# Moving a tile's query transpose, and a new batch's pooling, to other slots of a hand-written order

## The chip, the cores and the metric

The kernel runs on one core of a Trainium2 chip. The metric is device time in microseconds (us), the median of several executions. A core has engines that run side by side, each through its own instructions in order: TensorE (PE in the profile, with its weight loads as PEld), VectorE (DVE), ScalarE (ACT), GpSimd (POOL) and SyncE (SP). SP and POOL issue the DMAs of this kernel. An instruction that waits for a semaphore holds up whatever stands behind it on its engine, and that is true of a DMA's issue as well.

## What is computed

Attention over pooled keys and values, then a mixture of four experts over its output. Keys and values are averaged over groups of 8 rows, so 576 queries of a head see 72 keys.

```python
# q, k, v: (8 batches, 8 heads, 576 tokens, 64)
k_p = k.reshape(B, H, Sp, pool, D).mean(axis=3)      # Sp = 72
v_p = v.reshape(B, H, Sp, pool, D).mean(axis=3)
scores = scale * np.matmul(q, k_p.transpose(0, 1, 3, 2))
scores = scores - np.max(scores, axis=-1, keepdims=True)
attn = np.exp(scores)
attn = attn / (np.sum(attn, axis=-1, keepdims=True) + 1e-09)
x = np.matmul(attn, v_p)                             # heads side by side: (4608, 512)

p = domain_probs / (domain_probs.sum(-1, keepdims=True) + 1e-09)
for e in range(4):
    h = np.maximum(x @ w1[e], 0.0)                   # 512 -> 1024
    out += p[:, e:e + 1] * (h @ w2[e])               # 1024 -> 512
```

## The kernel before

**Tiles, groups, steps.** The 4608 tokens are 36 tiles of 128; four tiles make a group of 512, nine groups in all. A batch has 4.5 tiles, so some tiles hold rows of two batches. A *step* s is one expert of one group (36 steps). The main loop (line 603) walks through the steps, twelve *slots* each. In every three slots, two make an eighth of the hidden layer of step s+1 (`up`, four matmuls each, line 429) and one makes the output of one tile of step s (`down`, eight matmuls, line 462, followed by `collect` on DVE, which scales and adds into `acc`, and after the last expert stores `acc` from SP, line 485).

**The attention in the gaps.** The attention of later tiles is hung onto the slots by a plan, a dictionary from a slot's number to functions. At a slot the loop first emits the matmuls of the slot and then the planned functions, in the order in which they were put in. The schedule is manual: this emission order is the order on every engine. For a tile t of group g = 2 to 8 (t = g*4 + i), `base = (4g - 5 + i) * 12`, so successive tiles are twelve slots apart. `plan_tile(t, base - 2, turn)` puts in:

- `turn_q` at `base - 2 + turn`: `qT`, the transposed queries, by a transposing DMA from SP (line 290) that reads `qrow`; for t = 8 `turn` is 0;
- `scores` and `less_max` at `base`: the matmuls of line 306 with `qT` and the batch's `kT`, then on DVE the maximum (line 317) and the subtraction (line 319);
- `expo` on ACT (line 329) and `attn_T` at `base + 1`: `attnT`, the transposed probabilities, by a transposing DMA from SP (line 368);
- `sums` at `base + 2`: three DVE instructions (lines 350 to 353);
- `context` at `base + 6`: x's product (line 386) with `attnT` and the batch's `vbd`, then `x_sb` on DVE (line 392), then a transposing DMA from SP to `xT` (line 406), which the up-projection of the tile's group reads;
- `gate` at `base + 6`: POOL copies one element of `x_sb` (line 501), so that what stands behind it on POOL leaves only then; behind it `load_q` of tile t + 4 (line 107).

Tiles 0 to 7 are transposed on TensorE in place of by DMA.

**A new batch.** `plan_batch(b, slot)` is called for the first tile that holds rows of batch b (tiles 9, 13, 18, 22, 27 and 31 for batches 2 to 7), before that tile's `plan_tile`. It puts in `prep_k` (four DVE instructions: two folds at line 225, one at 232, the masked copy `kpad` at 240), `prep_kT` (a transposing DMA from SP, line 249) and `prep_v` (five DVE instructions, to `vbd`). The raw keys and values of batch b + 2 are loaded by POOL (lines 79 and 83) at slot `base + 6` of that tile and of the next, so behind `gate` and `load_q`.

Of the kernel before, what the change touches and what calls it, by code (L numbers as in the profile page):

```python
# [17 lines left out]
def kernel(  # L18
# [23 lines left out]
    TPG = G // P  # L42
# [104 lines left out]
    for sign, base in ((1, 0), (-1, SP - 1)):  # L147
        nc.gpsimd.affine_select(
            out=own[:], in_=own[:], compare_op=ALU.is_ge, fill=0.0,
            base=base, channel_multiplier=sign,  # L150
# [133 lines left out]
    def by_dma(t):  # L284
        return t >= 2 * TPG
# [202 lines left out]
    SLOTS = 12  # L488
    plan = {}

    def at(slot, fn, *args):
        plan.setdefault(slot, []).append((fn, args))

    def plan_batch(b, slot):
        at(slot, prep_k, b)
        at(slot + 4, prep_kT, b)
        at(slot + 8, prep_v, b)


    def gate(t):  # L500
# [2 lines left out]
    def plan_tile(t, slot, turn=0):  # L503
        exp, norm, move, sum_v = (3, 4, 3, 8) if by_dma(t) else (4, 5, 8, 10)
        if t + TPG < NT and not by_dma(t):
            at(slot, load_q, t + TPG)
        at(slot + turn, turn_q, t)
        at(slot + 2, scores, t)
        at(slot + 2, less_max, t)
        at(slot + exp, expo, t)  # L510
        at(slot + move, attn_T, t)
        at(slot + norm, sums if by_dma(t) else normalise, t)
        at(slot + sum_v, context, t)
        if by_dma(t):
            at(slot + sum_v, gate, t)
            if t + TPG < NT:
                at(slot + sum_v, load_q, t + TPG)
# [10 lines left out]
    for g in range(2, NG):  # L528
        for i in range(TPG):
            t = g * TPG + i  # L530
            base = (E * g - 5 + i) * SLOTS
            last_b = ((t + 1) * P - 1) // S
            if last_b >= done_batches:
                plan_batch(last_b, base - 13)
                done_batches += 1
                if last_b + 2 < B:
                    waiting += [(load_k, last_b + 2), (load_v, last_b + 2)]
            plan_tile(t, base - 2, -4 if t > 2 * TPG else 0)
            if waiting:
                load, b = waiting.pop(0)  # L540
                at(base + 6, load, b)
# [103 lines left out]
```

## Time and profile before

| | |
|---|---|
| time, median of 3 runs | 561.85 us (561.16 to 562.88) |
| the profiled execution: its time | 563.63 us |
| its span on the core | 561.7 us |
| granted TensorE clock, mean | 0.996 |
| `up` matmuls, line 429 | 271.8 us busy, 379 ns each |
| `down` matmuls, line 462 | 269.9 us busy, 379 ns each |
| query transposes on SP, line 290 | 27, median 3.8 us from issue to landing |
| probability transposes, line 368 | 28, median 2.6 us |
| x transposes, line 406 | 28, median 2.5 us |
| key transposes, line 249 | 6, median 2.6 us |
| loads of raw keys, 512 KB (POOL) | 7, median 8.1 us |
| loads of raw values, 512 KB (POOL) | 8, median 8.6 us |

The profile is one execution. For each engine it has what ran when, and the idle time in front of an instruction with the one whose end released it. A busy time is a sum over an engine's instructions; a wait counts for the whole only where the engine that waits sets the pace. The chain that ended last is followed back from the last instruction, at each step to what released it. For a DMA, "to landing" runs from its issue to its last completion.

### The profile page before, as it was taken

Reading aid. Unit: us, or ns where it says so; the run is one execution under the profiler, and the core shown is the slowest. Engines: PE = TensorE matmul, PEld = TensorE weight load, DVE = VectorE, ACT = ScalarE, POOL = GpSimd, SP = SyncE. Lnnn points to the kernel's source line nnn. Section 1 sums busy time; section 2 is a strip of 40 time slices with the busy share of each in tenths; the row PEclk is TensorE's granted clock in tenths of the full one; section 3 lists DMA queues with packets and bytes.
Section 4 is the critical chain, followed back from the end, with each engine's and each line's share of the span. In section 5 each row is a group of like instructions: output and inputs, shape, how many; then the busy total and the mean of one; then the engine's idle time right before and its main releaser. Section 6 shows DMA issues by size and latency. Waiting matters only on the chain.

```text
span 561.7 us, 7210 instructions
## 1 busy us (share of the span) xinstructions
PE 533.6 (95%) x2837; PEld 259.4 (46%) x2892; DVE 267.7 (48%) x458; ACT 210.8 (38%) x352; POOL 71.8 (13%) x121
## 2 busy tenths in 40 slices
PE   3799999999999898998999899999999999999997
PEld 1564554444444344444444344444444444444443
DVE  5865856444644445543563344744474444422222
ACT  1555553333333333333333233333333333333330
POOL 7224311210111000121011100110010000000000
PEclk9899999999999999999999999999999999999999
DMA  9999995544545335376535553334332331110001
GB/s 141 207 204 200 203 103 127 78 61 65 109 69 74 62 75 83 40 83 84 102 56 78 78 101 58 53 40 79 73 46 35 77 68 29 25 47 37 1 0 75
DMA packets 110688, 45.30 MB, mean 81 GB/s; under 512 B 87584, under 2 KB 106016, under 8 KB 110656
## 3 DMA queue, kind: packets, MB, share of 16 engines
q0 software_dynamic: 52512, 22.55, 32.8%
q1 hardware_dynamic: 58144, 22.30, 17.7%
q8 instruction: 22, 0.36, 0.3%
q14 instruction: 10, 0.08, 0.0%
HBM read 45.16 MB, written 9.44 MB: 97 GB/s over the span
## 4 chain that ended last, share of the span: by engine, by line
PE 88%; DMA 7%; DVE 2%; issue 1%; ACT 1%; POOL 0%; DVEq 0%; POOLq 0%
PE o_ps L462 41%; PE h_ps L429 40%; DMA qT<-qrow 5%; PE sc L306 2%; PE x_ps L386 2%; PE h_ps L445 2%; DMA kraw<-in_k_dram 1%; DMA attnT<-attn 1%; PE x_ps L412 1%; DVE kraw L225 0%; ACT attnT L373 0%; PE qT_ps L296 0%; PE o_ps L551 0%; POOL kraw L79 0%; DVE mx L317 0%
## 5 line engine op out<-in xcount | busy, mean ns | idle before, releaser
L433 ACT ACTIVATE h_sb<-h_ps 128x512 bf16<-128x512 f32 x280 | 166.5, 597 | 297.1 <-PE h_ps L429 290.6
L429 PE MATMUL h_ps<-xT,w 128*128 128x512 bf16 x1088 | 271.8, 379 | 1.5
L462 PE MATMUL o_ps<-w,h_sb 128*128 128x512 bf16 x1129 | 269.9, 379 | 1.4
L462 PEld LDWEIGHTS <-h_sb 128*128 128x128 bf16 x1152 | 112.3, 98 | 133.5
L477 DVE SCALAR_TENSOR_TENSOR acc<-o_ps,p_sb,acc 128x512 f32<-128x512 f32 x108 | 80.9, 749 | 179.0 <-PE o_ps L462 176.3
L429 PEld LDWEIGHTS <-w 128*128 128x128 bf16 x1120 | 105.9, 98 | 116.8
L501 POOL COPY gated<-x_sb 1x1 bf16<-1x1 bf16 x28 | 7.8, 278 | 370.6 <-DVE x_sb L392 370.6
L473 DVE TENSOR_SCALAR acc<-o_ps,p_sb 128x512 f32<-128x512 f32 x36 | 27.0, 749 | 58.3 <-PE o_ps L462 58.3
L317 DVE TENSOR_REDUCE mx<-sc 128x8 f32<-128x576 f32 x36 | 27.2, 754 | 19.3 <-PE sc L306 19.3
L107 POOL DMA_DIRECT2D qrow<-in_q_dram x36 | 30.4, 846 | 21.6 <-DMA w<-in_moe_w_dram 11.5
L319 DVE TENSOR_TENSOR d_sb<-sc,mx 128x576 f32<-128x576 f32 x36 | 27.3, 757 | 1.2
L392 DVE SCALAR_TENSOR_TENSOR x_sb<-x_ps,rs 128x512 bf16<-128x512 f32 x28 | 19.4, 692 | 16.4 <-PE x_ps L386 16.4
L329 ACT ACTIVATE attn<-d_sb 128x576 bf16<-128x576 f32 x28 | 19.1, 682 | 13.2 <-DVE d_sb L319 10.8
L306 PE MATMUL sc<-kT,qT 128*128 128x144 bf16 (+1 forms) x160 | 15.3, 230 | 7.6 <-DMA qT<-qrow 6.8
L350 DVE TENSOR_REDUCE es<-attn 128x8 f32<-128x576 bf16 x28 | 20.9, 745 | 0.5
L306 PEld LDWEIGHTS <-qT 128*128 128x128 bf16 (+1 forms) x160 | 10.7, 101 | 17.9 <-DMA qT<-qrow 9.7
L386 PEld LDWEIGHTS <-attnT 128*128 128x128 bf16 (+1 forms) x155 | 11.6, 100 | 9.1 <-DMA attnT<-attn 3.1
L386 PE MATMUL x_ps<-vbd,attnT 128*128 128x192 bf16 (+5 forms) x155 | 14.2, 231 | 1.5 <-DMA attnT<-attn 1.5
L225 DVE TENSOR_TENSOR kraw<-kraw 128x1280 bf16<-128x1280 bf16 (+5 forms) x18 | 10.8, 599 | 3.0 <-DMA kraw<-in_k_dram 2.7
L225 DVE TENSOR_TENSOR vraw<-vraw 128x1280 bf16<-128x1280 bf16 (+1 forms) x16 | 10.4, 652 | 0.2
L255 PE MATMUL kT_ps<-ident,kpad 128*128 128x128 bf16 x10 | 1.2, 264 | 9.3 <-DVE kpad L240 9.3
L445 PE MATMUL h_ps<-xT,w 128*128 128x128 bf16 x128 | 9.3, 240 | 0.7 <-ACT xT L418 0.7
(61 smaller groups left out, 153.4 us busy)
## 6 DMA issues: line engine op xcount, KB each, us to landing
out_dram<-acc SPq DMA_DIRECT2D x36, 256.0 KB, 2.0
vraw<-in_v_dram POOLq DMA_DIRECT2D x8, 512.0 KB, 8.6
w<-in_moe_w_dram POOLq DMA_DIRECT2D x8, 512.0 KB, 16.4
w<-in_moe_w_dram POOLq DMA_DIRECT2D x4, 1024.0 KB, 16.7
kraw<-in_k_dram POOLq DMA_DIRECT2D x7, 512.0 KB, 8.1
qrow<-in_q_dram POOLq DMA_DIRECT2D x28, 128.0 KB, 4.1
kraw<-in_k_dram POOLq DMA_DIRECT2D x2, 256.0 KB, 4.0
kraw<-in_k_dram POOLq DMA_DIRECT2D x8, 64.0 KB, 7.5
```

The source lines that it names most:

```text
L107: nc.gpsimd.dma_start(out=qrow[t][at:at + n], in_=q[b][:, tok:tok + n, :].rearrange("h p d -> p h d"),)
L225: nc.vector.tensor_add(out=rows[:, i0:i1, 0:w], in0=rows[:, i0:i1, 0:w], in1=rows[:, i0:i1, w:2 * w],)
L306: nc.tensor.matmul(sc[at:at + n, pair // 2, (pair % 2) * PW:(pair % 2 + 1) * PW], lhsT=qT[t][:, pair, at:at + n], rhs=kT[b][:].rearrange(" ...
L317: nc.vector.reduce_max(out=mx[:], in_=view, axis=AX.X)
L319: nc.vector.tensor_tensor(out=d_sb[:], in0=view, in1=mx[:].unsqueeze(3).to_broadcast([P, 2, 4, SP]), op=ALU.subtract,)
L350: nc.vector.reduce_sum(out=es[:], in_=e, axis=AX.X)
L386: nc.tensor.matmul(ps[at:at + n, h0 * D:(h0 + c1 - c0) * D], lhsT=attnT[t][:, i, at:at + n], rhs=flat[:, c0 * D:c1 * D], start=(i == 0), s ...
L429: nc.tensor.matmul(ps[:], lhsT=w1_sb[e][:, kc, fb * P:(fb + 1) * P], rhs=xT[g][:, kc, :], start=(kc == 0), stop=(kc == KC - 1),)
L433: nc.scalar.activation(out=hs[s][:, fb, :], in_=ps[:], func=ACT.Relu)
L462: nc.tensor.matmul(ps[:], lhsT=hs[s][:, fb, i * P:(i + 1) * P], rhs=w2_sb[e][:, fb, :], start=(fb == 0), stop=(fb == FB - 1),)
L473: nc.vector.tensor_scalar_mul(out=accs[t][:], in0=ps[:], scalar1=p_sb[:, e, t:t + 1])
L477: nc.vector.scalar_tensor_tensor(out=accs[t][:], in0=ps[:], scalar=p_sb[:, e, t:t + 1], in1=accs[t][:], op0=ALU.mult, op1=ALU.add,)
```

## The change

```diff
     def plan_batch(b, slot):
-        at(slot, prep_k, b)
-        at(slot + 4, prep_kT, b)
-        at(slot + 8, prep_v, b)
+        at(slot + 5, prep_k, b)
+        at(slot + 8, prep_kT, b)
+        at(slot + 9, prep_v, b)
...
             if last_b >= done_batches:
-                plan_batch(last_b, base - 13)
+                plan_batch(last_b, base - 2 - SLOTS)
...
-            plan_tile(t, base - 2, -4 if t > 2 * TPG else 0)
+            plan_tile(t, base - 2, -9 if t > 2 * TPG else 0)
```

In slots counted from the tile's `base`:

| what | slot before | slot after | stands behind, in the slot after |
|---|---|---|---|
| `turn_q` of tile t (t = 9 to 35) | base - 6 | base - 11 | `attn_T` of tile t - 1 |
| `prep_k` of a new batch | base - 13 | base - 9 | (`sums` of tile t - 1 are at base - 10) |
| `prep_kT` | base - 9 | base - 6 | `context`, `gate`, `load_q` of tile t - 1 |
| `prep_v` | base - 5 | base - 5 | (`context` of tile t - 1 is at base - 6) |

The instructions are the same in number and kind. The orders of TensorE, ScalarE and GpSimd are the same as before. On DVE the four instructions of `prep_k` stand behind the maximum, the subtraction, one collect and the three sums of tile t - 1, ahead of which they stood. On SP the order for a tile was attnT, xT, then the next tile's qT, and is attnT, the next tile's qT, then xT; for a new batch kT, which stood between attnT and xT, stands behind xT.

## The prediction

> **What bounds the kernel now.** I read the page first, for the engine that sets the pace.
>
> ```profile
> PE 533.6 (95%) x2837; PEld 259.4 (46%) x2892; DVE 267.7 (48%) x458; ACT 210.8 (38%) x352; POOL 71.8 (13%) x121
> PEclk9899999999999999999999999999999999999999
> ```
>
> TensorE is busy for 95% of the span at an almost full granted clock; no other engine reaches half. The change takes no matmul away, so it can only win TensorE's idle time. The second view is TensorE's waits from 85 us on, just before the first instruction that the change moves. The columns are the idle time in all, how often, and the longest.
>
> ```profile
> PE sc L306 <- DMA qT<-qrow: 6.8, 5, 2.2
> PE x_ps L386 <- DMA attnT<-attn: 1.5, 1, 1.5
> ```
>
> So all that the change can win on TensorE in this execution is 6.8 + 1.5 = **8.3 us**: five times the scores waited for their transposed queries, once x's product for its transposed probabilities. The third view, the chain that ended last (start, duration, what), gives the places:
>
> ```profile
> 164.15 5.12 DMA qT<-qrow
> 179.09 6.96 DMA qT<-qrow
> 219.34 4.34 DMA attnT<-attn
> 255.20 6.33 DMA qT<-qrow
> 300.71 5.46 DMA qT<-qrow
> 316.06 6.76 DMA qT<-qrow
> ```
>
> For a DMA, the duration is from issue to landing. The median query transpose lands in 3.8 us by the table of issues; these five took 5.1 to 7.0. The timeline around the longest says with what they collide, and how much time they had:
>
> ```profile
> 176.48 0.50 PE L386 MATMUL x_ps<-vbd,attnT 128*128 128x128 bf16 x5
> 177.80 1.19 SPq L406 DMA_TRANSPOSE xT<-x_sb  x1
> 178.42 0.92 POOL L107 DMA_DIRECT2D qrow<-in_q_dram  x1 [0.33 <-issue]
> 179.09 1.21 SPq L290 DMA_TRANSPOSE qT<-qrow  x1
> 179.32 0.76 POOL L79 DMA_DIRECT2D vraw<-in_v_dram  x1
> 186.10 0.42 PE L306 MATMUL sc<-kT,qT 128*128 128x144 bf16 x4 [2.22 <-DMA qT<-qrow]
> ```
>
> SP reaches the query transpose only when x_sb exists, since xT stands ahead of it; the same x_sb opens POOL's gate, so a query load and, in eight tiles, a load of raw keys or values leave at that moment. Each of the five late transposes has such a load beside it. Without the 2.22 us wait the scores would have begun at 183.88, so a transpose issued there has 183.88 - 179.09 = 4.8 us; the same subtraction at the other four gives 4.7 to 4.9. I take 4.7.
>
> **The change, part by part.** Tile t's scores stand at slot `base`; a step of twelve slots lasts 14.40 us in the undisturbed stretch from 113.50 to 127.90.
>
> *Queries moved (27 transposes, t = 9 to 35).* turn_q goes from base-6, behind xT of tile t-1, to base-11, behind attnT of tile t-1. On SP it passes xT and the output stores that stood between; its count and its 1.2 us of SP stay. In the undisturbed tile after 99.10, attnT is issued at 99.10 and xT at 104.77. A query transpose issued at 100.4 has landed by 102.8 if it takes the 2.4 us of the last two transposes (462.8 and 477.1), which have no load beside them; its scores come near 110.8. Even 6.96 us would be in time. Its other conditions are met early: qrow is loaded three tiles ahead, and its buffer was last read two tiles ago. For t = 9 qrow landed by 68.84 + 9.3 = 78.1 (the loads of that stretch took 8.1 to 9.3 us), before 86.34. **Gain: 6.8 us.** What now stands behind the query transpose on SP is the output stores and xT; xT is due 5.7 us after attnT, while the two issues take 2.4, so it waits for nothing new.
>
> *Keys' pooling moved (6 batches).* prep_k's four DVE instructions go from base-13, ahead of less_max of tile t-1, to base-9, behind its sums. By form they cost
>
> ```profile
> L225 DVE TENSOR_TENSOR kraw<-kraw 128x1280 bf16<-128x1280 bf16 x7 | 5.7, 817 | 2.4 <-DMA kraw<-in_k_dram 2.4
> L225 DVE TENSOR_TENSOR kraw<-kraw 128x640 bf16<-128x640 bf16 x7 | 3.4, 492 | 0.2
> L232 DVE TENSOR_TENSOR k_sum<-kraw 128x320 bf16<-128x320 bf16 x8 | 2.6, 325 | 0.3
> L240 DVE TENSOR_TENSOR kpad<-k_sum,mask_k 128x640 bf16<-128x640 bf16 x8 | 3.9, 492 | 0.3
> ```
>
> 817 + 492 + 325 + 492 ns = 2.1 us. Ahead of less_max they made attnT of tile t-1 late: normally x's product starts 103.52 - 99.10 = 4.4 us after attnT's issue, but at 219.34 the margin was 4.34 + 0.05 - 1.50 = 2.9. With 4.4 restored, even that slow 4.34 us landing fits. **Gain: 1.5 us.** The cost behind the sums: after 99.10 these end 2.15 us later (101.25), four instructions make 103.4, the collect behind them (0.75) 104.1, and x_sb started at 104.05. It is late by 0.1 us and xT with it; TensorE waits for neither until a group's first up-projection, six slots on. Each collect frees its bank more than a slot before the second next down-projection. Price 0.
>
> *Keys' transpose moved.* prep_kT goes from base-9 to base-6, so on SP behind xT of tile t-1: the very place and company that the query transpose leaves. TensorE's scores of the batch's first tile queue behind it, with 4.7 - 0.1 = 4.6 us. No row shows kT there. The query transposes of those six tiles are the nearest: 3.7, 3.5, 3.9, 3.9, 4.1 and 3.6 us, the slowest being
>
> ```profile
> L290 SPq DMA_TRANSPOSE qT<-qrow x1: 1205/1205/1205, 361.4 to 361.4; - x1
> DMA to landing us min/median/max: 4.1/4.1/4.1
> ```
>
> kT has 640 columns against 512. Lower bound: 0.2 more (2.6 against 2.4 unhindered), all within 4.6, cost 0. Upper: all of it by 640/512, so 4.6, 4.4, 4.9, 4.9, 5.1, 4.5, cost 0.3 + 0.3 + 0.5 = 1.1. I take **-0.3**, nearer to the lower row. No key or value load leaves there: these leave in the first two tiles of batches 2, 3, 4 and 5, behind kT.
>
> *Values.* prep_v keeps base-5, behind x_sb in DVE's order before and after: 0.
>
> *attnT with a query transpose right behind it.* The trace has the pair: kT was issued right behind attnT, or behind one store, in six tiles. attnT landed in 2.7, 2.6, 4.3, 2.6, 2.6 and 2.6 us, against a median of 2.6; so a follower costs 0. If attnT did land only with its follower, it would be 2.6 + 1.3 = 3.9 us, still under 4.4. One rule speaks against the change: the Trainium skill's page "DMA: Bandwidth & Descriptors", in its section "Queues, rings and completion order", says that a ring is consumed in order but a later descriptor may finish its write first, so that completion is not first in, first out. Five of the six rows do not show it; by the rule taken at its worst attnT's margin falls to 0.5 us and the sum stays at -8.0.
>
> *What comes sooner.* Where a stall goes, the next attnT is issued that much earlier, while the load still runs: for 179.32 at 188.86 - 2.22 = 186.6, the load's end (187.8) being 1.1 us away. Even if attnT moved nothing until then it would land in 1.1 + 2.6 = 3.7; at 325.62 the same sum gives 4.3, under 4.4. Two attnT already run so, landing in 2.8 and 4.0 us. Price 0.
>
> **Sum**: -6.8 - 1.5 + 0.3 = **-8.0 us**. The profiled execution took 563.63 us (span 561.7 and 1.93 around it), so it would be 555.6. It lies 1.8 above the median of the three runs, 561.85; that may be stalls that the others lacked, which would leave 6.2. I take the whole: **553.9 us**.
>
> **The rivals.**
> 1. *The stalls are smaller outside the profiled execution.* For it: those 1.8 us. Against it: the five collisions are in the program's order, not chance. With half of the gain: 557.9.
> 2. *attnT becomes the late transpose.* In 27 tiles attnT shares with its follower. It takes over from a landing of 4.4 us, and eats the gain at 4.4 + 8.3/27 = 4.7. For it: the row with 4.34 has a follower. Against it: the other five. Time then: about 561.9, no change.
> 3. *kT takes over the stall, slower.* Place: six first tiles' scores. If kT met a load as the worst query transpose did, 6.96 + 0.2 - 4.6 = 2.6 us each, 15.4 in all, less 8.3: 569. It decides from a landing of 4.6 + 8.3/6 = 6.0 us. For it: it is bigger and sits behind xT. Against it: the six rows end at 4.1, with a query load alone beside them.
>
> **How the numbers follow.** The forecast gets 0.83, rival 1 0.08, rival 2 0.06, rival 3 0.03. The range: low 552.4, when runs without the profiler lose 1.2 us more to these collisions than the trace shows; high 557.4, from 553.9 with kT's upper bound (+0.8), the 1.8 us between the runs, and most of the way to rival 1. Counting 0.3% (1.7 us) as what can be told from no change: faster 0.91, same 0.06, slower 0.03.
>
> **What would show it.** Right: no wait of the scores for qT; qT landing near 2.5 us, between attnT and xT; kT landing under 4.6; attnT still near 2.6; x_sb late by 0.1 us at most in six tiles; TensorE idle after 85 us below 0.5 us. Wrong: waits of L306 for kT, of L386 for attnT in most tiles, or a late query load that holds qT and, behind it on SP, xT.

## The result, and the profile after

The changed kernel takes **554.0 us** (median of 4 runs, 553.56 to 555.25), against 561.75 us for the kernel before beside it. The ratio is 0.9863, with a 95% interval from 0.984 to 0.9887. The forecast was 553.9 us, in a range from 552.4 to 557.4. The profiled execution took 555.25 us with a span of 553.2; before it was 563.63 with a span of 561.7. So the span fell by 8.5 us, where the sum had said 8.0.

The page of the changed kernel, in the lines that matter (engine totals, then the granted clock by slices, then the chain's shares, then the scores' group, with its idle time behind the bar):

```profile
PE 533.0 (96%) x2837; PEld 260.0 (47%) x2892; DVE 266.9 (48%) x458; ACT 212.0 (38%) x352; POOL 71.9 (13%) x121
...
PEclk9899999999999999999999999999999999999999
...
PE 94%; DMA 2%; DVE 1%; issue 1%; ACT 1%; POOL 0%; ACTq 0%; POOLq 0%
...
L306 PE MATMUL sc<-kT,qT 128*128 128x144 bf16 (+1 forms) x160 | 15.5, 231 | 0.4 <-ACT qT L300 0.3
```

TensorE's busy time is nearly what it was, 533.0 against 533.6 us, so most of the 8.5 us is idle time that is gone (the size is taken up again below, where the prediction is judged). The chain that ended last, which before went five times through a query transpose, now runs through TensorE for 94% of the span. The scores' idle time over the whole span is 0.4 us, before the first tile that the change touches. The view of TensorE's waits from 85 us to the end held two lines before; for the changed kernel it has none.

The timeline around the tile of the longest wait (start, duration, engine and line, operation, in brackets the idle time before it) shows the new order, and that the loads are still there:

```profile
172.53 1.21 SPq L368 DMA_TRANSPOSE attnT<-attn  x1
173.84 1.21 SPq L290 DMA_TRANSPOSE qT<-qrow  x1
...
176.94 0.50 PE L386 MATMUL x_ps<-vbd,attnT 128*128 128x128 bf16 x5
...
178.26 1.19 SPq L406 DMA_TRANSPOSE xT<-x_sb  x1
...
178.88 0.92 POOL L107 DMA_DIRECT2D qrow<-in_q_dram  x1 [0.33 <-issue]
...
179.78 0.76 POOL L79 DMA_DIRECT2D vraw<-in_v_dram  x1
...
184.18 0.41 PE L306 MATMUL sc<-kT,qT 128*128 128x144 bf16 x4
```

The query transpose leaves at 173.84, ten microseconds ahead of its scores and 4.5 ahead of the gate. The load of raw values still leaves behind x_sb, but now only xT is in flight beside it, which nothing awaits for at least six slots more. The scores follow with no wait.

The landing times of SP's transposes are in the views by tile (number of issues; the time on SP in ns; then least, median and greatest from issue to landing). The queries' of the changed kernel:

```profile
L290 SPq DMA_TRANSPOSE qT<-qrow x27: 1188/1205/1252, 87.0 to 462.8; - x27
...
DMA to landing us min/median/max: 2.4/2.4/4.1
```

Its keys':

```profile
L249 SPq DMA_TRANSPOSE kT<-kpad x6: 1267/1267/1278, 92.5 to 410.4; - x6
...
DMA to landing us min/median/max: 3.9/4.0/4.2
```

Its probabilities':

```profile
L368 SPq DMA_TRANSPOSE attnT<-attn x28: 1200/1202/1777, 85.6 to 475.9; - x28
...
DMA to landing us min/median/max: 2.6/2.6/2.9
```

Queries went from a median of 3.8 to 2.4 us, keys from 2.6 to 4.0: kT has taken over the place beside the gated loads. attnT kept its 2.6 with a query transpose right behind it in nearly every tile.

### The profile page after: what moved, and what is told of

The parts are those of the page before. It is cut to its first block, busy times and chain, and to the rows that moved or that the text cites. A ratio compares the mean times of both kernels' runs of the same rounds, so it can differ in the third digit from the quotient of the medians.

```text
span 553.2 us, 7201 instructions
## 1 busy us (share of the span) xinstructions
PE 533.0 (96%) x2837; PEld 260.0 (47%) x2892; DVE 266.9 (48%) x458; ACT 212.0 (38%) x352; POOL 71.9 (13%) x121
## 4 chain that ended last, share of the span: by engine, by line
PE 94%; DMA 2%; DVE 1%; issue 1%; ACT 1%; POOL 0%; ACTq 0%; POOLq 0%
PE o_ps L462 44%; PE h_ps L429 43%; PE x_ps L386 2%; PE sc L306 2%; PE h_ps L445 2%; DMA qg<-in_q_dram 2%; PE x_ps L412 1%; PE qT_ps L296 0%; ACT attnT L373 0%; POOL kraw L79 0%; ACT qT L300 0%; DVE vraw L225 0%; PE at_ps L372 0%; DVE qrow L545 0%; DVE vbd L270 0%
```

## The experiments

Times are medians in us; the ratio is to the kernel before in the same set of runs. The last column is TensorE's waits from 85 us on, in the profiled execution.

| run | edit | time | ratio, 95% interval | waits of TensorE |
|---|---|---|---|---|
| changed kernel | | 554.0 | 0.9863, 0.984 to 0.9887 | none |
| e1 | queries alone | 554.92 | 0.9878, 0.9859 to 0.9897 | attnT 1.5 |
| e9 | the same again | 554.73 | 0.9857, 0.9826 to 0.9888 | attnT 1.4 |
| e2 | pooling alone | 560.35 | 0.9983, 0.9955 to 1.0011 | qT 5.3 |
| e3 | queries one slot earlier than before | 553.97 | 0.9855, 0.9835 to 0.9875 | kT 0.4 |
| e4 | raw keys loaded beside kT | 564.42 | 1.0051, 1.0025 to 1.0077 | kT 6.8 |
| e5 | before, without eight raw loads | 554.7 | 0.9876, 0.9845 to 0.9907 | attnT 1.4 |
| e6 | before, once more | 565.12 (1 run) | | qT 7.3, attnT 1.4 |
| e7 | kT ahead of xT | 553.3 | 0.9834, 0.9803 to 0.9865 | none |
| e8 | changed kernel once more | 553.75 | 0.9839, 0.9805 to 0.9873 | none |

**e1 and e9: the queries' move alone.** From the kernel before:

```diff
-            plan_tile(t, base - 2, -4 if t > 2 * TPG else 0)
+            plan_tile(t, base - 2, -9 if t > 2 * TPG else 0)
```

> Only turn_q moves (base-6 to base-11); prep_k, prep_kT stay as before. Theory (query transposes collided with the raw loads): no wait of the scores for qT, 6.8 us of idle TensorE gone; the 1.5 us wait for attnT of tile 17 may stay, since prep_k still stands ahead of less_max. 553.5 to 556.0 us. Rival (the pooling's move brings the larger part): 559 us or more.

Measured: 554.92 us. All waits for qT are gone, and the one for attnT of tile 17 stayed (the waits of e1: total, times, longest):

```profile
PE x_ps L386 <- DMA attnT<-attn: 1.5, 1, 1.5
```

e1 is 0.9 us above the changed kernel, but the runs were not of one set, so I ran both again beside each other.

> Only turn_q moved, once more, beside the changed kernel on one chip. Theory (the pooling's move takes away the wait for attnT of tile 17): 1.0 to 1.5 us above the changed kernel, and that wait again at 1.2 to 1.6 us. Rival (the pooling's move is worth nothing): within 0.4 us of it.

> The changed kernel once more, on the chip of the two runs beside it: 553.3 to 554.8 us, no wait of TensorE after 85 us of 0.5 us or more, kT at 3.8 to 4.3 us.

Measured: 554.73 and 553.75 us, and their runs do not overlap (554.31 to 555.13 and 553.36 to 554.13). The difference is 0.98 us, just under the band that I gave; the profile of e9 has the wait at 1.4 us. The pooling's move is worth about 1 us of the time, the queries' move the rest.

**e2: the pooling's move alone.** The changed kernel with `turn_q` back at base-6:

```diff
-            plan_tile(t, base - 2, -9 if t > 2 * TPG else 0)
+            plan_tile(t, base - 2, -4 if t > 2 * TPG else 0)
```

> Only prep_k and prep_kT move; turn_q stays at base-6, so in six tiles SP issues xT, kT, then qT. Theory: the 1.5 us wait for attnT goes, the five waits for qT stay (6.8 us), and in the six first tiles of a batch qT is issued 1.3 us later, so has 3.4 us for a landing of 3.5 to 4.1 or a little more: 0.1 to 1.5 us each, 1 to 8 us in all. 561.5 to 568 us, so not faster than before. Rival (the pooling's move helps by itself): 560.3 us.

Measured: 560.35 us, just what I had put down for the rival. The waits:

```profile
PE sc L306 <- DMA qT<-qrow: 5.3, 5, 2.1
```

The wait for attnT is gone and the five tiles beside raw loads are still late, as expected. None of the six first tiles of a batch joined them, and that was my mistake: I moved the issue by 1.3 us and kept the landing at 3.5 to 4.1 us. In these six tiles qT, issued behind kT, landed 3.4, 3.0, 3.4, 3.2, 3.3 and 3.2 us after its issue, within the 3.4 us it had. The likely reason, which was not tried by itself, is that a landing that is long for a load beside it gets shorter when the issue comes later and the load is further along; delay and landing may not be added. The interval of the ratio holds 1.0, so the pooling's move alone can't be told from no change by these runs.

**e3: how early the queries must go.** The changed kernel with `turn_q` at base-7:

```diff
-            plan_tile(t, base - 2, -9 if t > 2 * TPG else 0)
+            plan_tile(t, base - 2, -5 if t > 2 * TPG else 0)
```

> The changed kernel with turn_q at base-7 in place of base-11: one slot earlier than before, and just ahead of xT on SP. Theory (what matters is that the issue on SP no longer waits for x_sb and does not leave with the loads behind the gate): nothing holds SP between attnT and qT but the output stores of every fourth step, so qT leaves as early or up to 5 us later, and the time is that of the changed kernel within 0.3 percent: 553 to 555.5 us, no wait of the scores. Rival (it is the five slots that matter): part of the 6.8 us comes back, 556 us or more.

Measured: 553.97 us, that of the changed kernel. One slot is enough, since what counts is which side of xT the issue stands on: SP does not know slots, it goes on as soon as the instruction in front is issued. There is one small exception, in SP's own timeline of e3 at the first new batch:

```profile
83.84 1.28 SPq L368 DMA_TRANSPOSE attnT<-attn  x1
85.18 3.96 SPq L485 DMA_DIRECT2D out_dram<-acc  x2
89.18 1.22 SPq L290 DMA_TRANSPOSE qT<-qrow  x1
90.44 1.27 SPq L406 DMA_TRANSPOSE xT<-x_sb  x1
91.75 1.70 SPq L249 DMA_TRANSPOSE kT<-kpad  x1
```

Here two output stores, which wait for their collects, stand ahead of qT. The query transpose then holds xT (6.6 us after attnT in place of 5.7 in the changed kernel), xT holds kT, and the scores wait 0.4 us for kT. So the place right behind attnT keeps 0.4 us, once, that the place ahead of xT alone does not.

**e4: raw keys beside kT.** The changed kernel; the keys of batch b+2 leave at base-6 of batch b's first tile:

```diff
                 if last_b + 2 < B:
-                    waiting += [(load_k, last_b + 2), (load_v, last_b + 2)]
+                    at(base - 6, load_k, last_b + 2)
+                    waiting += [(load_v, last_b + 2)]
```

> The changed kernel with the raw keys of batch b+2 loaded at base-6 of batch b's first tile, in place of base+6, so that this load leaves together with kT (four batches). Theory (a key or value load beside it is what makes a transpose late; kT has 4.6 us): the four kT beside a load land in 5.3 to 7.2 us instead of about 4.0 and the scores wait 0.7 to 2.6 us each, 3 to 10 us in all: 557 to 564 us. Rival (the loads are not the cause, or kT is safe at this place): kT at 4.0 to 4.6 us and 553 to 555 us.

Measured: 564.42 us, slower than the kernel before. The waits:

```profile
PE sc L306 <- DMA kT<-kpad: 6.8, 4, 2.3
```

The four kT that met a load (window from 85 to 300 us), against 3.9 to 4.2 in the changed kernel:

```profile
L249 SPq DMA_TRANSPOSE kT<-kpad x4: 1267/1272/1278, 91.4 to 289.6; - x4
...
DMA to landing us min/median/max: 5.5/6.9/7.3
```

The timeline of the third shows the same picture as the query transpose before the change:

```profile
228.61 1.19 SPq L406 DMA_TRANSPOSE xT<-x_sb  x1
...
229.86 1.27 SPq L249 DMA_TRANSPOSE kT<-kpad  x1
...
230.17 0.76 POOL L79 DMA_DIRECT2D kraw<-in_k_dram  x1
...
236.67 0.41 PE L306 MATMUL sc<-kT,qT 128*128 128x144 bf16 x4 [1.97 <-DMA kT<-kpad]
```

The load is what makes the transpose late, and this was the forecast's slower rival made real: with the key loads one tile earlier, the change would have lost. The time rose by 10.4 us over the changed kernel, more than the 6.8 of waits; most of the rest is the clock, below.

**e5: before, without the raw loads.** The kernel before, with nothing put into `waiting`:

```diff
                 if last_b + 2 < B:
-                    waiting += [(load_k, last_b + 2), (load_v, last_b + 2)]
+                    pass
```

> The kernel before, without the loads of raw keys and values of batches 4 to 7 (eight loads of 576 KB are left out; these batches pool again what lies in the buffers). Theory (these loads make the five query transposes late): every qT lands in under 4.7 us and the scores never wait for it; the wait for attnT of tile 17, which has no such load near it, may stay: 553.5 to 556 us. Rival (qT is late because it stands behind xT and beside the query load): waits of 3 us or more stay, 558 us or more.

Measured: 554.7 us. In the order of before, behind xT and beside the query load, the scores never wait for a query transpose any more. The queries' view by tile of e5:

```profile
L290 SPq DMA_TRANSPOSE qT<-qrow x27: 1188/1206/1286, 90.3 to 468.0; - x27
...
DMA to landing us min/median/max: 2.4/3.7/4.7
```

The median of 3.7 us is that of before, so xT and the query load together cost 1.3 us of landing and no time; the landings of 5.1 to 7.0 us needed the raw load. The wait for attnT stayed at 1.4 us.

**e6: before, once more.**

> The kernel before once more, for its profile. Theory (the stalls lie in the program's order): the same five waits of the scores, 6 to 7.5 us in all; the 1.5 us wait for attnT of tile 17 comes back within 0.7 us if the instruction fetch beside it is at a fixed place of the program, and not if it is chance. Rival (the profiled execution had stalls by chance, which the other runs lack): the five waits differ by more than half.

Measured, in its waits:

```profile
PE sc L306 <- DMA qT<-qrow: 7.3, 6, 2.4
PE x_ps L386 <- DMA attnT<-attn: 1.4, 1, 1.4
```

The five came back, and so did tile 17's attnT. The stalls lie in the order of the program. A sixth wait of 0.4 us was new: tile 21's query transpose, which no raw load stands beside, took 5.2 us; it took 4.7 in the first profile, and what slows it was not looked into.

**e7: kT ahead of xT.** The changed kernel with `prep_kT` one slot earlier:

```diff
-        at(slot + 8, prep_kT, b)
+        at(slot + 7, prep_kT, b)
```

> The changed kernel with prep_kT at base-7 in place of base-6, so that SP issues kT ahead of xT. Theory (a transpose issued before the gate opens meets no load): kT lands in 2.6 to 2.7 us in place of 3.9 to 4.2, the scores never wait, and the time stays at 553.3 to 554.8 us, since TensorE has no wait left to win after 85 us; x_sb and xT unchanged. Rival (kT waits for kpad on SP and holds xT, or more is to be won): over 555.5 or under 552.5 us.

Measured: 553.3 us (552.94 to 554.25, beside 553.75 for the changed kernel). Four kT landed in 2.6 us and two, on which I had not reckoned, in 3.4. The keys' view by tile of e7:

```profile
L249 SPq DMA_TRANSPOSE kT<-kpad x6: 1200/1202/1236, 89.2 to 406.0; - x6
...
DMA to landing us min/median/max: 2.6/2.6/3.4
```

It can't be told from the changed kernel in time, since TensorE has no wait left to give. What it buys is margin: in the changed kernel the first kT lands at 92.51 + 4.2 = 96.7 and its scores begin at 97.3.

## Why the prediction was right

**The 6.8 us of the query transposes.** All of it came, and e1 and e9 show it alone. e5 and e4 show the cause from both sides: take the raw loads away and no transpose is late in the old order; put a raw load beside kT and kT is late in the new one.

The prediction said of each late transpose that a raw load stood beside it; that is true, but not the whole condition. Eight query transposes had one, and three of them were in time: those issued at 106.06, 120.52 and 240.75 us landed in 4.5, 4.1 and 4.2 us. The second of these, with its load:

```profile
120.52 1.21 SPq L290 DMA_TRANSPOSE qT<-qrow  x1
...
121.25 0.78 POOL L79 DMA_DIRECT2D vraw<-in_v_dram  x1
```

In these three the raw load left 0.67 to 0.73 us behind the transpose, in the five late ones 0.16 to 0.23 us behind (179.09 and 179.32 in the prediction's timeline). The eight divide in the same way in e2 and e6 (3.8 to 4.0 us to landing against 5.1 to 7.1), and the four late kT of e4 had their load 0.27 to 0.33 us behind them. So it was the load that left almost at once that hurt. The distance was not varied by itself.

**The 1.5 us of attnT.** It came with the pooling's move and not without it (e1, e9, e2). In time it is worth 0.98 us. The step said that attnT's slow landing of 4.3 us would fit into a restored margin. The margin was restored (in the changed kernel x's product of that tile starts 4.4 us after attnT's issue), but it was not needed, since the slow place moved. In e1, e5, e6 and e9 the attnT issued there landed in 4.2 to 4.3 us. In the changed kernel attnT of that tile takes 2.6 and the query transpose behind it 4.1 (4.2 in e8), where there is time to spare. In the kernel before, an instruction fetch stands in the DMA rows between 217 and 225 us. In ten of the eleven profiles the first transpose in flight there when the fetch starts took 4.0 to 4.3 us; in e2, where none was in flight, attnT took 2.6; other fetches met transposes that landed in 2.4 to 2.6 us. That the fetch is the cause was not tried.

**The kT step, priced at 0.3 us, cost nothing.** It landed in 3.9 to 4.2 us, on the lower of the two bounds (the query's rows and 0.2 us), not on the upper one (those rows by 640/512). The slack of 4.6 us was right: the changed kernel has 97.3 - 92.5 = 4.8.

**The steps priced at zero** held. In the changed kernel attnT with a follower lands in 2.6 to 2.9 us, so rival 2 had no row to stand on. x_sb in the new batches' tiles is not late: xT leaves 91.28 - 85.61 = 5.7 us after attnT at the first of them, and it is 5.7 at the other five.

**Rival 1** fell: the five stalls came back in e6, and the medians differ by 7.75 us, not by half of the gain. Its row had, in part, another reason. The profiled execution of before lay 1.8 us above the median, and I read that as stalls which other runs might lack. Part of it is the granted clock. In the windows view of before, the columns after the window are its length, five engines' busy time, the clock, and the DMA's share and rate:

```profile
20.90:24.30 3.40, 3.20 (x31) 3.20 (x31) 2.45 (x6) 1.43 (x3) 0.00 (x0) 0.50 1.24 206
```

3.4 us at half the clock do the work of 1.7. It is the 8 among the slices of the clock in the first fence of the prediction, which I passed over as "almost full". The changed kernel's profiled execution has the same 8. The runs show the size: the changed kernel's four have a span of 553.2 us at a mean clock of 0.995, 552.3 at 0.997, and 551.5 twice at 1.000; the runs of before beside e7 to e9 have 560.7 to 562.0 at 0.996 and 557.6 to 559.3 at 1.000. How much of the 1.8 us it makes stays open: the scores of tile 8 start at 81.91 in this profile, and at 80.6 to 81.4 in the seven profiles without such a stretch in the head, the part ahead of these scores.

**The size of the sum, 8.0 us, has some luck in it.** Ahead of the scores of tile 8 TensorE does nothing that the change touches. They start at 81.91 us before and at 82.86 in the changed kernel. From there to the end the profile shrank from 479.8 to 470.3 us, so by 9.5; the head was 0.95 longer, which makes the 8.5 of the spans. The idle time that the prediction added up is 8.3 of these 9.5. The other 1.2 is in TensorE's busy time, 464.99 us before and 463.77 after in this stretch, 0.2 for each of the six waits. A likely reason: a matmul is shown with 379 ns, but in the chain eight of them take 1.73 us, 0.22 each, and where TensorE stops behind one, the 0.16 us between the two is lost as well and counts as busy. Against that, the medians fell by 7.75 us, 1.8 less than this stretch of the two profiles; how much of that is smaller stalls outside the profile is open. The two departures nearly cancel.

**Rival 3** had the right price and point: in e4 the worst kT landed in 7.3 us, against 7.16 in the rival, and the third waited 1.97 us for a landing of 6.67, so it had 4.7. Its premise, a load beside kT, is not in this order.

## What to carry to other kernels

A DMA's place in a hand-written order is set by what its queue must issue first and by what else leaves at that moment, not by its slot: one place past the instruction that waits was worth as much here as five slots. Before moving a transfer, look for the slowest landing of its kind, name the transfer beside it, and check that the one which takes over the vacated place has the slack: here kT had 0.6 us left. Compare the granted clock of two executions before reading a difference between them as stalls.

## What was not expected of the hardware

**A wait of TensorE can cost more than its length.** In e6 the wait of 2.38 us that ends at 185.67 is followed by a stretch at half the clock. The windows before it, in it and behind it:

```profile
178.70:186.00 7.30, 4.86 (x26) 2.19 (x25) 1.50 (x2) 1.79 (x3) 1.32 (x3) 1.00 1.01 123
186.10:189.50 3.40, 3.40 (x9) 1.20 (x8) 1.51 (x2) 1.17 (x2) 0.00 (x0) 0.51 0.04 6
189.60:193.00 3.40, 3.40 (x17) 1.53 (x16) 1.79 (x4) 1.19 (x2) 0.00 (x0) 1.00 0.25 48
```

Nine matmuls in 3.4 us, then seventeen: the wait of 2.4 us lost 1.7 more. In e4 two of the four waits, of 2.33 and 2.08 us, were followed by the same, here with the window ahead of each:

```profile
95.68:99.09 3.41, 1.08 (x8) 0.47 (x7) 0.56 (x1) 0.60 (x1) 0.00 (x0) 1.00 1.11 181
99.10:102.51 3.41, 3.41 (x9) 1.22 (x8) 1.51 (x2) 1.17 (x2) 0.00 (x0) 0.50 0.42 120
...
157.12:160.53 3.41, 1.33 (x10) 0.49 (x9) 0.75 (x1) 0.60 (x1) 0.00 (x0) 1.00 1.14 204
160.54:163.95 3.41, 3.41 (x11) 1.39 (x11) 1.52 (x2) 0.93 (x2) 0.00 (x0) 0.50 0.36 108
```

It is not every time: 2.22 us in the kernel before and 2.11 in e2 left the clock at full. What tells the cases apart is where a wait falls on a grid of windows of equal length. The half-clock stretches of e4 begin at 20.59, 99.10 and 160.54 us, which is 23 and 18 times 3.413 us apart, and each lasts one such window. Each of the three waits above lies within one window (in e6 the wait from 183.29 to 185.67, in the window from 182.72 to 186.13), and the window behind it has half the clock. The longest wait of the kernel before is cut in two by the grid (its windows begin 47 and 48 times 3.413 us after the stretch at 20.90):

```profile
181.33:184.74 3.41, 2.56 (x12) 0.97 (x10) 0.75 (x1) 1.20 (x2) 0.00 (x0) 1.00 1.19 154
184.74:188.15 3.41, 2.05 (x13) 1.11 (x14) 1.51 (x2) 0.60 (x2) 0.00 (x0) 1.00 0.41 64
```

Neither window is idle for more than 1.4 of its 3.41 us. From the scores of tile 8 to the last matmuls, in all eleven profiles, the three windows with 2.1 us of idle time or more are each followed by half the clock, and no other window is; the largest idle time that left it at full is 1.6 us. In the head, with its smaller matmuls, 1.55 to 1.75 us were enough in four profiles, so the limit is not sharp in these numbers. This also makes e4's sum come out: from the scores of tile 8 to the end its profile is 11 us longer than that of e8 (481.4 against 470.3), near 6.8 of waits, two stretches of 1.7 and 0.16 for each of four stops, 10.8.

The Trainium skill's page "TensorE: Matmul & The Clock Gate" describes the gate in its section "Part 1: The HAM clock gate (the "warmup" mystery)": half rate after one idle window of about 3.4 us, full rate after a busy one, with windows that run freely, so that they do not start with the kernel. The length of the stretch and the grid agree with these rows (3.4 us at 0.50). The idle time that brings it on does not: 2.1 to 2.4 us within a window were enough in three of the profiled waits.

The kernels with waits of 2 us also scatter more: before from 559.64 to 565.24 in one set, e2 from 557.14 to 564.23, e4 from 561.74 to 569.63, against 553.36 to 554.13 for the changed kernel in e8. Each run has its span and mean granted clock on record, and the longest runs are at a low clock, the shortest at a high one: before 563.4 us at 0.993 and 557.6 at 1.000, e2 562.1 at 0.992 and 555.0 at 0.999, e4 567.5 at 0.987 and 559.6 at 0.999. A mean lower by 0.012 is worth 6.8 of e4's 7.9 us (0.012 of 563), and 0.007 is worth 3.9 of 5.8 in before and of 7.1 in e2. So the clock makes half of the scatter or more; the rest is open, since only one execution of each set has a trace.
